# S4 convolution gated with a GLU on one core: second-half weights read again from the inputs, late sums gathered in SBUF, and a new order of issue

## The chip, the cores and the metric

The kernel runs on one core of one Trainium2 chip. The metric is the time on the device of one execution, in microseconds, as a median over several runs. All inputs lie in the chip's memory when the time starts, and the whole output must lie there when it ends. The program uses five engines that each work through their own instructions in order: TensorE (PE, matrix products), VectorE (DVE), ScalarE (ACT), GpSimd (POOL, which here only issues transfers that add to what is in memory) and SyncE (SP, which issues all other transfers). A wait at the head of an engine's queue holds up everything behind it on that engine.

## The reference, cut to what matters

```python
x = A_u                                            # 1 x 2048 x 512
g = sigmoid((x * gate_w).sum(-1, keepdims=True))   # one gate per row
a = _A_ref(x, ...)     # S4: K[d, l] = Re sum_n C dt B exp(dt A l), then a causal convolution of x with K, + x * Dskip
b = _B_ref(x, ...)     # GLU: h = sigmoid(x Wg) * (x Wu), 512 -> 1792; b = h Wd, 1792 -> 512
return g * a + (1 - g) * b
...
def _B_ref(x, w_gate, w_up, w_down):
    g = einsum("bsd,df->bsf", x, w_gate)
    u = einsum("bsd,df->bsf", x, w_up)
    h = sigmoid(g) * u
    return einsum("bsf,fd->bsd", h, w_down)
```

## The kernel before, in words

All products keep nearly float32 accuracy: a float32 matrix is split into a high part that TensorE takes as it is (fp32r) and a low rest, and three products (high by high, high by low, low by high) take the place of one. `split` (L938) does it for one 128x512 piece: SP loads the piece into a buffer of the pool ST, ACT copies the high part (L946), DVE subtracts it to get the low part (L947).

**The GLU.** The 2048 rows are taken in two halves of 1024; each half is two blocks of 512 rows (`sb`). The 1792 inner columns are 14 slices of 128 (`f`), taken in four groups of 3, 4, 4 and 3 (`GROUPS`). `hidden` (L1025) makes for each half, block and slice two products into PSUM (tile gups, L1040, 24 matmuls of 128x512); `post` (L1077) takes the sigmoid (ACT, L1081), the product (DVE, L1083) and splits the result (ACT L1087, DVE L1088). `down` (L1093) multiplies a group of slices with the down weights (tile dps, L1110) for each of the 16 row tiles `t`; `add` (L1120) scales the sum of the group by 1 - g on ACT (tile part, L1124) and sends it to the output: the first group by a plain store on SP (L1127), the other three by a transfer on POOL that adds to what is there (L1129). A tile's buffer comes free when its transfer has landed.

The weights are loaded and split in the first half (`load_gu` L967, `load_dn` L998). Three slices of the gate and up weights (`KEEP`) and of the down weights stay in SBUF for the second half, which takes the slices in reverse. The other 11 slices are stored after their split to a scratch tensor wsp in memory (`keep`, L956), 1024 KB of gate and up weights and 512 KB of down weights each, and the second half loads them from there, already split (L993, L1020).

**The convolution.** ACT and DVE build the tables from which the convolution's kernel is made: sines and cosines (`angles` L473, `powers` L441), exponentials (`magnitudes` L492) and doubling by complex products (`double` L520, L533 to L535). `tables` (L539) multiplies them on TensorE (tile kps, L577; 16 blocks of 128 small matmuls), `second` transforms the result (wps, L607) and stores it. `rows` (L629) transforms the input. `passes` (L697) then runs twice, for the first and the second 256 of the 512 output columns (`j` = 0, 1): `ustep`, `kstep` and `inverse` (tiles s2u, s2k, ips) make the product in the transformed domain, `evict` copies it out and stores it to b_s, and `finals` and `last` (L851, L866) load it again, transform it back (fps, L876), take sums and differences on DVE, scale by g on ACT (L901) and add the result to the output with a transfer on POOL (L905). Once the tables are done, some of their memory joins the pools of the second pass (L711 to L714).

**The order.** Every engine's instruction stream is written out by a planner while the program is built: each piece of work is a generator, and the string `ORDER` (L63) names, letter by letter, whose turn is issued next and on which engine ("tables PE", "splitw DVE", "add POOL"). So `ORDER` fixes the order on every engine; the cost figures in the planner only decide which free buffer is taken.

Of the kernel before, what the change touches and what calls it, by code (L numbers as in the profile page):

```python
# [44 lines left out]
GROUPS = [3, 4, 4, 3]  # L45
HALF = L // 2
# [10 lines left out]
         "rows PE", "hidden PE", "down PE", "passes SP", "split ACT", "split DVE", "keepw SP", "splitw ACT",  # L57
         "splitw DVE", "keepd SP", "splitd ACT", "splitd DVE", "second DVE", "second -", "second PE", "second ACT",
         "second SP", "sort ACT", "dot DVE", "dot ACT", "urest ACT", "urest DVE", "urest SP", "post ACT",
         "post DVE", "add ACT", "add SP", "add POOL", "ustep -", "ustep PE", "ustep ACT", "ustep DVE",  # L60
# [3 lines left out]
    "ABBDcEEdGDfgZfBcdgZZZGVWqrWqrWqrWqXDcdZZXVrFAYVEfDcgdZEZDfgZcdsZHvHIJwIGsECDijNOKfgKLYVFEvcPNZZfgMZvdwwKiDcWqZZWjZqdDaWq"  # L64
    "vwvwFuMWqheXuPZPucdZPQZaMMvwZMKEEijaZuRRXQVMSeFQrsuZxrSSvwZZfEESQSfSKraSQyviwsuuZaZYVSNOPSsuaxyageSNPvSSKSgZSaaZvLPMxauK"
    "ZePMsMZaayuSwvSSYVSfEfMwWWSWTExUZZvZwvgjgGWuQMwqqKfRRZwvQhQQQTZpZvguEfEsgMfUNOsqPSpNPSZSZZwSgZvSPaSaaZwZSZqSyeSPQuHSwSvw"
    "xaZfEaaSklmRSRQQSQQuxaZnaSZaNOfEvwyvwZSZrxaZFZPauNgSanSyvwFijHPvSZPwTZfiXxUZjvPQeZhEEvZwIwRvJXVIuRQQQZQZwZYyFpaaasvZZviw"
    "vfNOPTwjafKNKLMKuGxzUhygZZPMPgZeZZwtogMPuMQgMKvwpaaaaEeMSkSSKSVSYSKRRSQSSEvZZQSQSSQfxzaaaZaSNlSHvZuEfsxzaaaaOuVSwWrsmPNx"
    "zaWaafaHEZWqSvSSwZLSTnhxzUuZeWPvqgPMKZPMMwvgQpZRaaaaRqwqXwQQQZQTgMxzMNuKnofgvZZhOEEUZPNpkaaaaMSwvZuhSSZPvwSZXSlmZZZPPSwS"
    "vxzaaQFZZfRRSSwSfgSSQQSFijvaaFuFQQSwvZZeNESrVnOnoivYwZiZZPsuSuNSZSvSTvewZwgExzPEifPZPjUQpZjvRaajwaaxzgIJhwIhHRQKQQsuQNKL"  # L70
    "vwuZOaaaaxzTVvfgZaaaaEZxzUYMfKZgPNZvpMaZMPhakaatwlMPPMtZxzQaaaKwMSSSSSSuaHmfKgRSKxzaauaSRQQuuSZZDDavwSnnDvwQcZxzadLMKara"
    "SQSNOobbbbbbDcdavrMZZxzaaZvFaaMPc0SwFvZZ1bbMZNPSZPSSPSSwSvTijMKxzwijdw2cUQv245abbRZbRbFbdw6bZZvZZQQDMvDQDQTwpDUNwrijSZOP"
    "4NSScdSp6aaSbc5SZbb6SZPPZbPQklSSvwZxzavZaSwSaR67mZRQQxzcacnaSZQSQSvaSn8v!Z!$$xzaaaNZOPZSdvNSSSTwd0xPdZw!!$$z1bbPPUpZaaaQ"
    "ZIR3JoZ345bbbwbxzbaaabv4IKKZERwQLbxzaavMQQvZQNTOKaPZ5bhxU6MzZvEwN6MpaaaZP6PMPMxklmaaaZwQZvKMSSS6nSSSwSn78wKSSRSbZ!b!$$Zx"
    "aaaSZRQrxvQaaQ0wvQ!wS!Zva1bbw$xZZ2ZvNOSaPwZ$KaSvZyFy245bbbb4ZbZbawbyEESNPvSPSZSwZLMSTvKP6wxUyMovM5bbbM6pQR6RZZa6Z78!ZwQM"
    "vZ!$$rQQQNaaTZvxUOPKNZMSSSSSSZwvpaaaPSPwPwSZvZzQ#Sklvxaa#w0$SamRSZxRSQQyEnnZaQFSwyQvZN$a1bbZwry2vaFx24ZFZvZwZ5bbSbaZZOP4"
    "wvSaNwPPaS6SS6PvSZTaZExz56UQp6bRERQQQ7QZaaaax8!!$$ZvwTaaaaZxovUw#ypkl!$$zZmnnaZaZv9999%aawwo9b999%bbZZx&ab)bb0)b)ZbabaaZ"
    "Z(&)(*Z*(bzb(xaa**aba)19z9vwb99%bbvwEvZZvZw)wxa2zaa2(45bb40b(6vw*ZaxZ65bbbz*(v(*z6&)))bbbZZ6Zvwa(F(**b*a1F9939bwZZZZ7(9("
    "**vwvw2a8F!!$$b#4ZaxFvZvw!$wv5baZb0Z%b66wa4&)b))56b6b$EbZaax(Zv(**b((**bzbazba1a2baxz3456wv7aabaa8!xz!$6!b0$Zaa4Z!b$$b56"
    "6ab7aZ1xzaw22aabax8!#!!ab4a566b4EaazZvx$b$566aa$aZax78z!w#Z$ZaE#$a$!vzaa$wZZ$FFZ99999vwZZxza%vwZvZ&w(9ZZav))((**9w9(%&)Z"  # L80
    "Fa)9vZ(**9)xZzw9a(a99%a&)(**(99(*x*a)z9%)&)(v(*Zv*a(w(**)ax)wZZZ(a(*Z*vw(v(*awva*azxawzaaaaaaaxaxazxzzaxz")

XLATE = 0
SLACK = dict(dma=1.6, eng=0.06)
FETCH = 6.5

# [1114 lines left out]
```

## Time and profile before

| | |
|---|---|
| median of 3 runs (653.32 to 656.91) | 654.02 us |
| the profiled execution | 657.56 us |
| its span, first to last instruction | 655.8 us |
| mean granted clock of TensorE | 0.971 |

The span is counted from the first to the last instruction of the profiled execution; 1.76 us of its time lie around it. Busy time of an engine is the time in which at least one of its instructions runs. A duration in a row is from the start of one instruction to its end, and neighbours overlap a little, so the distance between two starts is what one costs in a row of them. In the rows of a timeline the bracket at the end is the idle time before the instruction and what ended it. "wgu", "wdn" and "xt" are inputs, "wsp" is the scratch tensor.

### The profile page before, as it was taken

The page shows a single profiled execution, that of the slowest core. Times are in us where ns is not written, and L with a number is a line of the kernel's source. Part 1 is how long each engine was busy: PE and PEld are TensorE (multiplying, and loading weights), DVE is VectorE, ACT ScalarE, POOL GpSimd, SP SyncE. Part 2 cuts the span into 40 slices and gives each one's busy share as a digit, 9 for nine tenths or more (in the row PEclk, how much of TensorE's full clock was granted, in tenths as well). Part 3 has the DMA queues.
Part 4 walks back from the last instruction along what each step waited for, and adds up shares of the span by engine and source line. Part 5 has one row for each costly group of instructions (what it writes and reads, how often), then busy time and mean ns, then how long its engine had stood idle before and what let it go on. Part 6 is the DMA issues. An engine that isn't in the chain of part 4 may idle for free.

```text
span 655.8 us, 16738 instructions
## 1 busy us (share of the span) xinstructions
PE 599.2 (91%) x7136; PEld 454.4 (69%) x7136; DVE 518.2 (79%) x726; ACT 444.3 (68%) x668; POOL 70.3 (11%) x84
## 2 busy tenths in 40 slices
PE   3987989989989999998999999999799889899993
PEld 2564778867868787866777777777677557567672
DVE  6999999999999998999999999897324636452450
ACT  4696888988799889987988879876352232322341
POOL 0000000000100011100111000000013301311363
PEclk9799989999999999997999999999899989999997
DMA  7585581668828686964389469186599999999988
GB/s 239 173 320 182 196 275 65 198 219 252 224 69 244 226 225 163 246 132 122 49 188 278 98 172 335 37 250 184 162 258 252 263 286 230 241 296 262 247 108 115
DMA packets 96586, 132.50 MB, mean 202 GB/s; under 512 B 39936, under 2 KB 65408, under 8 KB 92672
## 3 DMA queue, kind: packets, MB, share of 16 engines
q1 hardware_dynamic: 84992, 114.65, 58.0%
q0 software_dynamic: 11520, 16.78, 17.5%
q8 instruction: 56, 0.92, 0.6%
q14 instruction: 18, 0.15, 0.1%
HBM read 67.97 MB, written 63.44 MB: 200 GB/s over the span
## 4 chain that ended last, share of the span: by engine, by line
PE 45%; DVE 17%; issue 12%; DMA 11%; ACT 6%; SPq 4%; POOL 4%; POOLq 0%; DVEq 0%; ACTq 0%
PE gups L1040 23%; PE dps L1110 11%; PE kps L577 4%; POOL out L905 3%; PE wps L607 2%; PE s2k L788 2%; DMA out<-mn 2%; DMA u<-xp 2%; DMA ak<-a_k 1%; DMA out<-part 1%; DMA out<-yt 1%; DVE t L533 1%; DVE sg L1083 1%; DVE T L535 1%; DVE T L534 1%
## 5 line engine op out<-in xcount | busy, mean ns | idle before, releaser
L1040 PE MATMUL gups<-x,gu 128*128 128x512 f32 x1344 | 341.0, 401 | 19.4 <-ACT gu L946 6.3
L1040 PEld LDWEIGHTS gups<-x,gu 128*128 128x128 f32 x1344 | 253.0, 192 | 92.5 <-issue 15.0
L1110 PE MATMUL dps<-dnw,h 128*128 128x512 f32 x672 | 174.3, 397 | 2.9 <-ACT part L1124 1.3
L1110 PEld LDWEIGHTS dps<-dnw,h 128*128 128x128 f32 x672 | 125.2, 189 | 38.9 <-issue 7.0
L1129 POOL DMA_DIRECT2D out<-part x48 | 42.6, 888 | 482.9 <-ACT part L1124 337.3
L1124 ACT ACTIVATE part<-dps,omg 128x512 f32<-128x512 f32 x64 | 43.6, 681 | 63.7 <-PE dps L1110 60.9
L1083 DVE TENSOR_TENSOR sg<-gups,sg 128x512 f32<-128x512 f32 x56 | 38.4, 687 | 22.0 <-PE gups L1040 19.9
L506 ACT ACTIVATE B<-B 128x32 f32<-128x32 f32 (+2 forms) x96 | 53.7, 673 | 0.3
L577 PE MATMUL kps<-B,T 128*32 128x64 f32 x2048 | 35.6, 231 | 15.3 <-DVE B L515 8.1
L577 PEld LDWEIGHTS kps<-B,T 128*32 128x32 f32 x2048 | 32.7, 118 | 22.2 <-issue 8.0
L1087 ACT ACTIVATE h<-sg 128x512 fp32r<-128x512 f32 x56 | 34.9, 626 | 16.5 <-DVE sg L1083 16.2
L533 DVE TENSOR_TENSOR t<-T,bz 128x1024 f32<-128x1024 f32 (+3 forms) x48 | 41.3, 861 | 1.5 <-ACT ez L436 0.9
L1088 DVE TENSOR_TENSOR h<-sg,h 128x512 fp32r<-128x512 f32 x56 | 38.4, 687 | 4.9 <-ACT h L1087 4.9
L535 DVE TENSOR_TENSOR T<-T,t 128x1024 f32<-128x1024 f32 (+3 forms) x48 | 41.4, 863 | 0.2
L534 DVE TENSOR_TENSOR T<-T,bz 128x1024 f32<-128x1024 f32 (+3 forms) x48 | 41.5, 864 | 0.0
L1081 ACT ACTIVATE sg<-gups 128x512 f32<-128x512 f32 x56 | 33.0, 593 | 6.5 <-DVE h L1088 4.2
L616 ACT ACTIVATE kev<-wps 128x1024 f32<-128x1024 f32 x16 | 31.0, 2006 | 5.5 <-PE wps L607 5.5
L798 DVE TENSOR_TENSOR tt<-s2k,uf 128x1024 f32<-128x1024 f32 x16 | 19.6, 1225 | 18.4 <-PE s2k L788 18.3
L431 ACT ACTIVATE af<-ex 128x1024 int32<-128x1024 f32 x16 | 16.9, 1059 | 13.3 <-DVE ex L484 13.3
L788 PE MATMUL s2k<-ak,wwk 64*32 64x256 f32 x512 | 19.2, 397 | 5.7 <-DVE ev L309 3.2
L901 ACT ACTIVATE yt<-yt,g 128x256 f32<-128x256 f32 x16 | 7.4, 502 | 24.7 <-DVE yt L894 24.7
L309 DVE COPY yt<-fps 128x512 f32<-128x512 f32 x7 | 4.8, 692 | 24.1 <-PE fps L876 17.3
(102 smaller groups left out, 730.8 us busy)
## 6 DMA issues: line engine op xcount, KB each, us to landing
out<-part POOLq DMA_DIRECT2D x48, 256.0 KB, 5.5
wsp<-gu SPq DMA_DIRECT2D x11, 1024.0 KB, 6.6
gu<-wsp SPq DMA_DIRECT2D x11, 1024.0 KB, 8.4
a_u<-evu SPq DMA_DIRECT2D x32, 256.0 KB, 4.8
a_k<-kev SPq DMA_DIRECT2D x8, 1024.0 KB, 6.7
au<-a_u SPq DMA_DIRECT2D x32, 256.0 KB, 6.6
ak<-a_k SPq DMA_DIRECT2D x32, 256.0 KB, 5.1
b_s<-ev SPq DMA_DIRECT2D x32, 256.0 KB, 4.3
```

Source lines behind the costliest of these rows:

```text
L506: A.activation(B[:, :, 0, 1 << k::2 << k], B[:, :, 0, 1:64 >> k:2], AF.Exp, scale=float(1 << k))
L533: yield "DVE", dve(n), lambda: V.tensor_tensor(t2, src, sb, op=OP.mult), [t, slot.t]
L534: te = yield "DVE", dve(n), lambda: V.tensor_tensor(dst, src, br, op=OP.mult), [t]
L535: te = yield "DVE", dve(n), lambda: V.tensor_tensor(dst, dst, t2[:, :, ::-1], op=OP.add), [te]
L577: mm(p[32 * jj:32 * jj + 32, s], T[:, 32 * i + ch, c], B[:, ch, c], start=(c == 0), stop=(c == 1), tile_position=(0, 32 * jj), skip_group_ ...
L1040: mm(p, gu[:, a, k, dc], x[:, b, dc], start=(dc + n == 0), stop=(dc == NC - 1 and n == 2))
L1083: t = yield "DVE", dve(512), lambda: V.tensor_tensor(sg, pu, sg, op=OP.mult), [t, tu]
L1087: t = yield "ACT", act(512), lambda: A.activation(h[:, 0], sg, AF.Copy), [t, hs.t]
L1088: t = yield "DVE", dve(512), lambda: V.tensor_tensor(h[:, 1], sg, h[:, 0].bitcast(F32), op=OP.subtract), [t]
L1110: mm(p, h[:, a, 128 * s:128 * s + 128], dn[:, b], start=(f == fs[0] and n == 0), stop=(f == fs[-1] and n == 2))
L1124: te = yield "ACT", act(512) + 0.1, lambda: A.activation(part, p, AF.Copy, scale=omg[:, t:t + 1]), [tp, gate[t, 1].t, ss.t]
L1129: ts = yield "POOL", kb(430), lambda: nc.gpsimd.dma_start(out[t], part, accum_op=OP.add), [te, begun[t]]
```

## The change

Four things are done together.

1. `keep` is gone, and so is wsp. In the second half the 11 slices that are not kept are loaded from the inputs again, three pieces of 256 KB a slice, and go through `split` as in the first half. `drop` no longer waits for a store.
2. For the row tiles 8 to 15 (the second half) a new generator `take` loads the output tile into an SBUF buffer `acc` once the first two groups and the first 256 columns of the convolution have been added in memory. The last two groups (`INTO` = 2) are then added to `acc` by one DVE instruction each, from PSUM, and the second 256 columns of the convolution by one DVE instruction for each tile. SP stores the finished tile. For these, the ACT scaling and the POOL transfer are gone. The other 32 + 24 POOL transfers stay.
3. The tables' memory joins the pools as several buffers rather than one each: TA as 2, KEV and EX as 2 each, KST as 2 buffers of ST, TB as the 8 buffers `acc`.
4. `ORDER` is a new string. The figures with which the planner counts transfers are new too.

```diff
+class Piece:
+    def __init__(self, slot, n, i): self.slot, self.n, self.i = slot, n, i
...
-                for n, s in (("big", TB[0]), ("big", KEV[0]), ("big", EX[0]), ("uf", TA[0]), ("ev", T2[0]), ("t", T2[1]),
-                             ("wwk", PG[0]), ("wwu", PP[0]), ("wwv", BZ[0])):
+                for n, s in (("ev", T2[0]), ("t", T2[1]), ("wwk", PG[0]), ("wwu", PP[0]), ("wwv", BZ[0])):
                     fin[n].join([s])
+                fin["uf"].join(pieces(TA[0], 2, [P, 2, 2, 2, W]))
+                fin["big"].join(pieces(KEV[0], 2, [P, 4, W]) + pieces(EX[0], 2, [P, 4, W]))
+                ST.join(pieces(KST[0], 2, [P, 512]))
+                ACC.join(pieces(TB[0], 8, [P, D]))
...
+    out_done = [Ev(INTO + 1) for _ in range(NM)]
+    held = [[Ev(), None] for _ in range(NM)]
+    oleft = [Ev(len(GROUPS) - INTO + 1) for _ in range(NM)]
+    late = lambda j, t: t >= 8 and j == NW - 1
+    def take(t):
+        yield out_done[t]
+        sl, = yield ACC, 1
+        a = held[t][1] = sl.tile("acc")
+        held[t][0].set((yield "SP", kb(256), lambda: S.dma_start(a, out[t]), [out_done[t].t, sl.t]))
+        yield oleft[t]
+        sl.free((yield "SP", kb(256), lambda: S.dma_start(out[t], a), [oleft[t].t]))
+
+    def gather(t, add, n, deps, slot):
+        yield held[t][0]
+        a = held[t][1]
+        te = yield "DVE", dve(n) + 0.06, lambda: add(t, a), deps + [held[t][0].t]
+        if slot is not None:
+            slot.free(te)
+        oleft[t].set(te)
...
             for t in range(4):
-                yield begun[4 * t4 + t]
+                yield held[4 * t4 + t][0] if late(j, 4 * t4 + t) else begun[4 * t4 + t]
...
+            if late(j, 4 * t4):
+                for i in range(2):
+                    yield from gather(4 * t4 + k[i], lambda t, a: V.scalar_tensor_tensor(
+                        a[:, cols], y[:, i], g[:, t:t + 1], a[:, cols], op0=OP.mult, op1=OP.add), W, [te], slot if i else None)
+                continue
...
-    def keep(done, stored, dst, src, size):
-        yield done
-        stored.set((yield "SP", (kb(size), 0.18 - 6e-5 * size), lambda: S.dma_start(dst, src), [done.t]))
...
-                else:
-                    yield wsent[f]
-                    t = yield "SP", (kb(1024), 0.1), lambda: S.dma_start(gf, ga), [gs.t, wsent[f].t]
...
+                for k in range(2):
+                    yield from split("splitw", wgu[f, :, 512 * k:512 * k + 512], gu[:, 0, k], gu[:, 1, k], gs, wready[half, f][0][k])
...
-                    dready[1, f][0].set((yield "SP", kb(512), lambda: S.dma_start(df, da), [ds.t, dsent[f].t]))
...
+                yield from split("splitd", wdn[f], dn[:, 0], dn[:, 1], ds, dready[half, f][0])
...
         yield gate[t, 1] if gi == 0 else added[t][gi - 1]
+        if t >= 8 and gi >= INTO:
+            yield from gather(t, lambda t, a: V.scalar_tensor_tensor(
+                a, p, omg[:, t:t + 1], a, op0=OP.mult, op1=OP.add), 512, [tp], bank)
+            added[t][gi].set(tp)
+            return
```

The two `ORDER` strings are too long to print. This is what they say of the turns that come before the last "tables PE" (the sixteenth block of small matmuls, kps), and of the whole string; turns that are not named have the same count in both.

| turn | ahead of the last kps, before | after | whole string, before | after |
|---|---|---|---|---|
| hidden PE (6 matmuls of 128x512) | 177 | 180 | 228 | 228 |
| down PE (3 matmuls of 128x512) | 148 | 144 | 224 | 224 |
| splitw ACT and DVE, each | 28 | 39 | 28 | 50 |
| splitd ACT and DVE, each | 14 | 18 | 14 | 25 |
| post ACT / post DVE | 85 / 83 | 86 / 85 | 112 / 112 | 112 / 112 |
| urest ACT / urest DVE (128x1024) | 13 / 3 | 16 / 0 | 13 / 3 | 16 / 0 |
| ustep ACT / ustep DVE (128x1024) | 6 / 2 | 8 / 0 | 12 / 4 | 13 / 3 |
| evict ACT / evict DVE (128x512) | 12 / 2 | 15 / 1 | 25 / 7 | 24 / 8 |
| add ACT | 43 | 42 | 64 | 48 |
| add POOL / last POOL | 25 / 0 | 26 / 0 | 48 / 32 | 32 / 24 |
| take SP, add DVE | 0 | 0 | 0 | 16 each |

ACT holds one set of functions at a time: sine, exponential and sigmoid are in three sets, copy and absolute value are in all. Followed through the strings, the ACT turns change from one set to another 58 times in the order before and 70 times in the order after, in both strings ahead of the last kps.

More of the change, by code (lines that the diff above doesn't have):

```diff
@@ L56 @@
          "mags DVE", "mags ACT", "tables DVE", "tables -", "tables PE", "rows -", "rows SP", "rows DVE",
[L57 to L60, printed above, removed]
+         "rows PE", "hidden PE", "down PE", "passes SP", "take SP", "split ACT", "split DVE", "splitw ACT",
+         "splitw DVE", "splitd ACT", "splitd DVE", "second DVE", "second -", "second PE", "second ACT", "second SP",
+         "sort ACT", "dot DVE", "dot ACT", "urest ACT", "urest DVE", "urest SP", "post ACT", "post DVE",
+         "add ACT", "add SP", "add POOL", "add DVE", "ustep -", "ustep PE", "ustep ACT", "ustep DVE",
          "kstep -", "kstep PE", "kstep DVE", "inv -", "inv PE", "finals SP", "evict ACT", "evict DVE",
@@ L161, in __init__ @@
     def __init__(self):
-        self.free, self.kind, self.last, self.strands, self.dma, self.adds = dict(SP=0.74, ACT=0.7, DVE=0.87), None, None, [], 0.0, 0.0
-        self.count, self.entered = 63.0, 0.0
+        self.free, self.kind, self.last, self.strands = dict(SP=0.74, ACT=0.7, DVE=0.87), None, None, []
+        self.count, self.entered, self.used = 63.0, 0.0, [0.0] * 1024
     def spawn(self, gen, kind):
@@ L298, in body @@
     dts = dr.tile([16, 32], F32, name="dts")
-    wsp = dr.tile([NF, P, 3072], F32, name="wsp")
     cst = ctx.enter_context(pool("cst"))
@@ L313, in body, with pieces @@
     XB = slots(ps, "xb", BANKS["xb"], [P, 2, 512])
+    def pieces(slot, n, shape):
+        parts = Slots(Slot(Piece(slot, n, i), None, shape, F32) for i in range(n))
+        for s in parts:
+            s.t = slot.t
+        return parts
     def release(slot, ev):
```

128 lines of the change are left out of this document (63 added, 65 removed).

## The prediction

> **What bounds the kernel now.** I begin with the page's summary and its slices.
>
> ```profile
> span 655.8 us, 16738 instructions
> PE 599.2 (91%) x7136; PEld 454.4 (69%) x7136; DVE 518.2 (79%) x726; ACT 444.3 (68%) x668; POOL 70.3 (11%) x84
> PE   3987989989989999998999999999799889899993
> DVE  6999999999999998999999999897324636452450
> ACT  4696888988799889987988879876352232322341
> DMA  7585581668828686964389469186599999999988
> ```
>
> Two parts can be seen. Up to slice 28, some 460 us, DVE is full, PE nearly so, and the transfers have gaps. Behind it DVE and ACT are half idle and the transfers fill every slice. The border is the last block of the tables' small matmuls (kps). The timeline shows it, and the view by stages, split there, puts numbers to the parts (columns: PE, PEld, DVE, ACT, POOL busy, clock, DMA share, GB/s). The next lines, on the transfers from 470 us on, say which queue fills them.
>
> ```profile
> 469.62 0.33 PE L577 MATMUL kps<-B,T 128*32 128x64 f32 x9 [3.97 <-issue]
> 0.00:470.00 470.00, 434.43 (x5451) 336.63 (x5452) 438.88 (x620) 384.68 (x565) 22.96 (x30) 0.98 0.66 192
> 470.00:656.00 186.00, 164.78 (x1686) 117.82 (x1686) 79.35 (x106) 59.59 (x103) 47.34 (x54) 0.95 1.02 228
> q1 hardware_dynamic: 35168, 32.25, 64.7%
> q0 software_dynamic: 7776, 9.96, 36.3%
> ```
>
> First part: DVE is idle 31.1 us of 470, so it sets this part's end, and ACT has 85.3 us to spare. Second part: SP's queue (q1) and POOL's adding transfers (q0) together take 101% of the 16 DMA engines. PE is the engine with most work there. What stopped it is the next question, answered by the waits of PE in that part, with two waits of DVE and ACT that stand ahead of them, the half-clock place in the timeline, and the tail.
>
> ```profile
> PE s2k L788 <- DVE ev L309: 3.2, 1, 3.2
> PE s2k L788 <- ACT ev L309: 2.1, 1, 2.1
> PE fps L876 <- DMA b_in<-b_s: 0.6, 2, 0.3
> PE dps L1110 <- DMA dnw<-wsp: 0.4, 1, 0.4
> PE s2k L788 <- DMA ak<-a_k: 0.4, 1, 0.4
> DVE ev L309 <- DMA out<-mn: 9.2, 1, 9.2
> ACT ev L309 <- DMA out<-mn: 6.1, 2, 4.1
> 536.68 1.96 PE L788 MATMUL s2k<-ak,wwk 64*32 64x256 f32 x32 [3.17 <-DVE ev L309]
> 540.02 4.01 PE L1040 MATMUL gups<-x,gu 128*128 128x512 f32 x12
> 545.53 1.07 PE L788 MATMUL s2k<-ak,wwk 64*32 64x256 f32 x32
> 637.55 6.87 PE L1110 MATMUL dps<-dnw,h 128*128 128x512 f32 x29 [0.23 <-DVE h L1088]
> 645.10 0.69 ACT L1124 ACTIVATE part<-dps,omg 128x512 f32<-128x512 f32 x1 [1.94 <-DMA out<-part]
> 649.31 0.87 POOL L1129 DMA_DIRECT2D out<-part  x1 [0.42 <-issue]
> ```
>
> The five waits of PE, 6.7 us, all have a late transfer behind them: the copies "ev" could not start because a buffer was held by an adding transfer (out<-mn) for 9.2 and 6.1 us. After the 3.17 us pause the s2k block took 1.96 us where the next took 1.07, and twelve matmuls at 540.02 took 4.01 us where a row below has 2.72. So the clock was halved from the pause to about 543 us, some 6.8 us, of which I count half as lost, 3.4 us (an estimate). Together 10.1 us are due to transfers. Then the tail: the last matmul ends at 637.55 + 6.87 = 644.4, the span at 655.8, 11.4 us later, since the last sums wait for a buffer (1.94 us) and then queue on POOL until 649.31.
>
> **The change part by part.** These rows give the prices: a matmul in a row of them, the split's two instructions, the copies that change their engine, the transfers.
>
> ```profile
> 454.04 2.72 PE dps L1110 x12
> L947 DVE TENSOR_TENSOR gu<-st,gu 128x512 fp32r<-128x512 f32 x28 | 19.0, 685 | 0.0
> L946 ACT ACTIVATE gu<-st 128x512 fp32r<-128x512 f32 x28 | 17.3, 626 | 1.7 <-issue 1.1 <-DMA st<-wgu 0.5
> 630.50 0.69 DVE L888 TENSOR_TENSOR mn<-fps,yt 128x512 f32<-128x512 f32 x1
> 631.10 0.68 DVE L889 TENSOR_TENSOR mn<-fps,yt 128x512 f32<-128x512 f32 x1
> L309 DVE COPY evu<-ups 128x1024 f32<-128x1024 f32 x3 | 3.7, 1219 | 0.0
> L309 ACT ACTIVATE evu<-ups 128x1024 f32<-128x1024 f32 x13 | 13.2, 1017 | 7.0 <-PE ups L661 7.0
> gu<-wsp SPq DMA_DIRECT2D x4, 1024.0 KB, 9.4
> dnw<-wsp SPq DMA_DIRECT2D x7, 512.0 KB, 7.4
> out<-part SPq DMA_DIRECT2D x16, 256.0 KB, 4.4
> out<-part POOLq DMA_DIRECT2D x8, 256.0 KB, 4.7
> L1081 ACT ACT_TABLE_LOAD x18 | 23.1, 1283 | 0.3
> 125.75 1.28 ACT L1081 ACT_TABLE_LOAD   x1
> 127.04 0.60 ACT L1081 ACTIVATE sg<-gups 128x512 f32<-128x512 f32 x1
> ```
>
> A matmul costs 2.72 / 12 = 0.227 us. A DVE instruction of 128x512 lasts 0.69 and starts 0.60 after its neighbour (630.50, 631.10), so I price it at 0.60, one of 128x1024 at 1.22 - 0.09 = 1.13, and an ACT copy of 128x512 at 0.626 - 0.09 = 0.53.
>
> *First part, DVE.* Counted in the order, 15 splits more stand ahead of the last kps: 15 x 0.60 = +9.0; two post turns more, +1.2; three urest and two ustep copies go to ACT, -5 x 1.13 = -5.7; one evict less, -0.6. Sum **+3.9 us** on the engine that sets the end of this part. Bounds: 0, if the 31.1 us of idle take it in, and +9 if the copies that leave gain nothing because DVE only waits there instead.
>
> *First part, ACT.* 15 splits x 0.53 = 8.0; five copies x 0.93 = 4.6; three evicts, one post, less one add, 1.6; and twelve more changes of function set at 1.283: 15.4. That is 29.6 us, from 384.7 to 414 of 470. I take **0**: 56 us of idle remain to cover it. If the cover is gone, DVE waits behind it; this is the third rival. The row speaks of what stands in front of the loads, 0.3 us of idle for 18, and the timeline of what follows: load at 125.75, sigmoid at 127.04. The Trainium skill (ScalarE: Activation LUTs, section "What ACT_TABLE_LOAD costs") also gives 1283 ns but adds a drain of about 1380 ns, 2.66 us a switch. By it the twelve switches would be 31.9 us, by the rows 15.4; the rows leave no gap for a drain, so the measurement decides.
>
> *First part, PE.* Ahead of the last kps three hidden turns more and four down turns less: 18 - 12 = 6 matmuls, which leave the second part: **-1.4 us** (0 to -1.4).
>
> *First part, stores.* 11 x 1.5 MB of stores to wsp vanish, on a DMA share of 0.66. DVE waits for hardly any transfer there, so 0.
>
> *Second part, transfers.* POOL loses 16 x 256 + 8 x 128 KB, 5.24 of its 9.96 MB: 36.3% x 0.53 = 19 points. The loads from wsp in this part (4 of gu, 7 of dnw: 7.9 MB) come to half: 3.9 / 32.25 x 64.7 = 8 points less. `take` adds 16 x 256 KB, 4.2 MB: 8 points more. So 101% fall to about 82%. Of the 10.1 us due to transfers I take two thirds away, **-6.7 us**, since the adds of the first 256 columns, which held "ev", stay on POOL. Bounds: 0 (the buffer is held just as long) and -10.1.
>
> *Second part, engines.* DVE gets 18 splits, 16 sums from PSUM and 8 of 128x256; the new instruction's nearest row is the 128x512 sum from PSUM above, so 34 x 0.60 + 8 x 0.33 = 23 us, on 79 of 186. PE, busy 164.8 of 186, covers that; uncovered it would be up to 23. ACT loses 16 scalings and gains 18 splits: even.
>
> *New waits.* Each sum of `gather` waits on DVE for the load of `take`, and behind it stand the products of `post`, for which PE's banks wait. The load can go out when three adds have landed. Seven of the eight loads stand at least 9 PE turns ahead of their sums in the order; the last add, load and sum stand at one place, 29 PE turns ahead of the end. I take 0, since queues may run ahead of the order's places; the bound is the landing of an add and of a load, 4.7 + 4.4 = 9.1 us, once. SP loses 22 stores and 22 loads and gains 33 loads and 16 takes: +5 issues, nothing.
>
> *Tail.* After the last dps come one DVE sum (0.7), an SP store (4.4 to landing) and what closes the program, which before took 655.8 - 649.31 - 4.7 = 1.8 (4.7 is the median landing of a POOL add in the last 56 us). With 0.2 to start, 7.1 in place of 11.4: **-4.3 us** (bounds 0, as some POOL adds still stand among the last turns, and -5.5).
>
> *Sum:* +3.9 + 0 - 1.4 - 6.7 - 4.3 = **-8.5 us** on the profiled execution, 657.56, of which the span is 655.8 and 1.76 lie around it: 649.1. The runs' median, 654.02, is 3.5 below that execution, so the forecast is **645.5 us**.
>
> **The rivals.** *All the waits go* (chance 0.21): with a fifth of the transfers gone, the five waits and the half clock vanish, and the 31.1 us of idle DVE in the first part take in its 3.9 us. -1.4 - 10.1 - 4.3 = -15.8: 638.2. For it speaks the full DMA row; against it that DVE was 93% busy.
>
> *Hidden anyway* (0.19): the waits for "ev" come from the buffer and not from the load on the DMA engines, and only the tail is gained: +3.9 - 1.4 - 4.3 = -1.8: 652.2. For it speaks that both waits name out<-mn, whose transfers of the first 256 columns stay.
>
> *ACT becomes the bound of the first part* (0.18): the twelve set changes fall between an ACT step and a DVE step of the same chain (sine, exponential, doubling), so each holds DVE by its 1.283 us. -8.5 + 15.4 = +6.9: 660.9. It turns the result slower when 11.8 of the 15.4 us are exposed. For it: DVE's waits for ACT were there before,
>
> ```profile
> DVE bz L466 <- ACT ey L461: 4.9, 3, 2.9
> DVE B L511 <- ACT B L506: 3.3, 2, 2.5
> ```
>
> against it: ACT waited far longer for DVE and PE, 85.3 us idle.
>
> **How the numbers follow.** The forecast has 0.42, the rivals 0.21, 0.19 and 0.18. A measurement of this kernel tells about 0.5% from no change: 650.75 to 657.3. Faster: forecast and first rival, 0.63; same: 0.19; slower: 0.18. The range goes to the first rival with its tail at the bound and some DVE idle gained, 633, and to the slower rival, 660, leaving out about one tenth on each side. The likeliest cases of one sign, 633 to 650.7, hold 0.6.
>
> **What would show it.** After: kps ends 2 to 6 us later than 470; DVE's waits for ACT ahead of it stay under 16 us; about 70 table loads; DMA share behind it near 0.85; the waits of s2k for ev shorter than 3.2 and 2.1 and the half clock gone there; last matmul to end of span about 7 us. Wrong if kps comes 10 us later with DVE idle for ACT (third rival), if the ev waits stay at 5 us (second), if DVE waits at the new sums for acc, or if the new order moves the border by more than its counts do: the counts say what is issued before what, not how well it interleaves, and that is the largest thing the trace of before cannot show.

## The result and the profile after

The changed kernel takes **632.9 us** (median; 630.66 to 635.37) against 653.67 (652.95 to 656.91) for the kernel before on the same chip: a ratio of 0.968, 95% interval 0.963 to 0.972. It is some 21 us faster where 8.5 were forecast, just past the low end of the range. A later set of runs (e14 below) gave 0.962 (0.956 to 0.967).

The profiled execution took 631.64 us. These lines of its page answer to those shown of before: the span, the busy times and the slices.

```profile
span 629.9 us, 16805 instructions
PE 594.3 (94%) x7136; PEld 449.9 (71%) x7136; DVE 543.2 (86%) x777; ACT 466.7 (74%) x695; POOL 49.4 (8%) x60
PE   4999899999979999996999999999999999989996
DVE  6899999999999999999999999999743767746467
ACT  4698989999998899999899899996943424321140
DMA  7714324247834754493786976732799999995985
```

The shape is the same: DVE full up to slice 28, the transfers nearly full behind it. PE does the same 7136 matmuls, but it starts at full pace in the second slice rather than the third and has fewer holes. To compare, I cut each execution at the start of the last kps block (the border) and at the end of the last matmul. The view by stages gives, for before and then for a second profile of it (e1 below): columns are PE, PEld, DVE, ACT and POOL busy, clock, DMA share, GB/s.

```profile
0.00:65.00 65.00, 46.90 (x252) 32.19 (x253) 57.49 (x113) 43.66 (x77) 0.20 (x4) 0.94 0.69 227
65.00:463.80 398.80, 385.30 (x5075) 302.46 (x5073) 380.00 (x506) 340.81 (x489) 22.76 (x26) 0.98 0.66 185
463.80:644.40 180.60, 167.00 (x1815) 119.80 (x1814) 80.74 (x108) 59.12 (x103) 44.74 (x51) 0.97 1.01 236
```

```profile
460.80:644.90 184.10, 169.62 (x1815) 119.99 (x1814) 80.72 (x108) 58.91 (x103) 44.73 (x51) 0.96 1.02 232
```

For the changed kernel, and a second profile of it (e14):

```profile
0.00:65.00 65.00, 55.48 (x271) 40.73 (x271) 55.84 (x106) 48.07 (x76) 0.20 (x4) 1.00 0.52 160
65.00:458.60 393.60, 378.09 (x5059) 293.28 (x5057) 382.63 (x523) 364.54 (x525) 22.75 (x26) 0.99 0.58 147
458.60:624.70 166.10, 160.68 (x1809) 115.86 (x1808) 102.85 (x148) 54.14 (x95) 26.42 (x30) 1.00 1.00 218
```

```profile
459.20:627.80 168.60, 162.12 (x1809) 116.74 (x1808) 103.01 (x148) 54.27 (x95) 26.40 (x30) 0.99 0.97 214
```

The spans are 655.8 and 655.1 before, 629.9 and 633.0 after; the tail is what is left of each behind the last matmul. So, with the mean of two profiles each:

| stage | forecast | before (two profiles) | after (two profiles) | change of the means |
|---|---|---|---|---|
| first part, to the border | +3.9 | 463.8, 460.8 | 458.6, 459.2 | -3.4 |
| second part, to the last matmul | -8.1 (-6.7 and -1.4) | 180.6, 184.1 | 166.1, 168.6 | -15.0 |
| tail | -4.3 | 11.4, 10.2 | 5.2, 5.2 | -5.6 |
| sum | -8.5 | | | -24.0 |

The medians differ by 20.8 us in the first set of runs and by 27.3 in the later one; the sum of the stages, from two profiles each, lies between. Every stage came out better than forecast: the first by 7 us, the second by 7, the tail by 1.

**The second part** can be taken apart from those rows. PE's idle time is the length less the busy time: 13.6 and 14.5 us before, 5.4 and 6.5 after, so -8.1. The rest is busy time, -6.9: 6 matmuls left this part (1815 to 1809), 1.4 us, and the clock rose from 0.97 and 0.96 to 1.00 and 0.99, worth 0.035 x 182 - 0.005 x 167 = 5.5 us (an estimate: the missing share of the clock times the length). The waits of PE behind the border in the changed kernel are few; these are the three largest (us in total, times, longest):

```profile
PE fps L934 <- DMA b_in<-b_s: 1.7, 2, 1.2
PE s2u L797 <- ACT ev L335: 1.5, 1, 1.5
PE s2k L824 <- DMA parts<-a_k: 0.7, 1, 0.7
```

The pause of 3.97 us with the cause "issue" inside the last kps block, which the prediction quoted and then did not count, is not there. The queues from 459 us on:

```profile
q1 hardware_dynamic: 37477, 31.83, 78.2%
q0 software_dynamic: 4464, 4.98, 19.3%
```

POOL's adding transfers fell from 9.96 to 4.98 MB as counted. But the two queues together still take 98% of the 16 engines in a stretch of 171 us: the work for the transfers fell from 1.01 x 186 = 188 us to 167, and the part shrank with it.

**The first part** was forecast to end later because DVE gets more work there. Its instructions ahead of the border rose by 10 (113 + 506 = 619, then 106 + 523 = 629), 11 by the count in the order. But its idle time fell from 463.8 - 437.5 = 26.3 us to 458.6 - 438.5 = 20.1, its busy time rose by 1 us where 3.9 were forecast, and the first 65 us hold 5 to 9 us more of PE's work (46.9 before and 48.9 in e1, 55.5 after and 54.3 in e14). The waits of DVE and ACT in this part say where the idle time went; first two of ACT's before (DVE's largest two, 4.9 and 3.3 us, stand in the prediction), then after.

```profile
ACT af L431 <- DVE ex L484: 13.3, 7, 4.3
ACT af L435 <- DVE ex L432: 9.3, 7, 2.9
```

```profile
DVE B L544 <- ACT B L539: 5.4, 2, 4.2
DVE sg L1116 <- PE gups L1073: 2.9, 1, 2.9
DVE gu L1011 <- ACT gu L1010: 2.2, 1, 2.2
...
ACT af L464 <- DVE ex L517: 4.6, 6, 2.3
ACT af L468 <- DVE ex L465: 3.3, 4, 1.9
```

ACT, in the chain of sines and exponentials (af, ex), waited 22.6 us for DVE before and 7.9 after, while it took on 12 more changes of function set (59 table loads in the trace of before, 71 after) and its busy time up to the border rose by 28 us (384.5 to 412.6). DVE's two largest waits for ACT come to 8.2 us before and 7.6 after.

**The tail**: the last sums are three DVE instructions in a row, and the last store follows.

```profile
623.64 1.07 PE L1143 MATMUL dps<-dnw,h 128*128 128x512 f32 x4
...
624.50 2.07 DVE L1156 SCALAR_TENSOR_TENSOR parts<-dps,omg,parts 128x512 f32<-128x512 f32 x3
```

The last matmul ends at 624.7, the last sum at 626.6, the span at 629.9. SP's stores of the finished tiles land within 2.1 us (median of 8):

```profile
out<-parts SPq DMA_DIRECT2D x8, 256.0 KB, 2.1
```

### The profile page after: what moved, and what is told of

Same layout as the page of the kernel before. It is cut to its first block, busy times and chain, and to the rows that moved or that the text cites. A ratio compares the mean times of both kernels' runs of the same rounds, so it can differ in the third digit from the quotient of the medians.

```text
span 629.9 us, 16805 instructions
## 1 busy us (share of the span) xinstructions
PE 594.3 (94%) x7136; PEld 449.9 (71%) x7136; DVE 543.2 (86%) x777; ACT 466.7 (74%) x695; POOL 49.4 (8%) x60
## 4 chain that ended last, share of the span: by engine, by line
PE 48%; DVE 23%; DMA 11%; ACT 8%; SPq 4%; issue 4%; POOL 0%; DVEq 0%; POOLq 0%
PE gups L1073 26%; PE dps L1143 12%; PE kps L610 3%; DVE t L566 2%; DVE T L567 2%; DMA b_in<-b_s 2%; DVE T L568 2%; PE wps L640 2%; PE s2k L824 2%; ACT B L539 2%; DMA parts<-a_u 2%; DVE B L548 1%; DMA parts<-wdn 1%; DVE B L544 1%; PE ips L859 1%
## 5 line engine op out<-in xcount | busy, mean ns | idle before, releaser
L1167 POOL DMA_DIRECT2D out<-part x31 | 27.7, 892 | 439.8 <-ACT part L1162 421.2
L1162 ACT ACTIVATE part<-dps,omg 128x512 f32<-128x512 f32 x47 | 31.9, 678 | 16.8 <-PE dps L1143 10.2
L1011 DVE TENSOR_TENSOR gu<-st,gu 128x512 fp32r<-128x512 f32 x48 | 32.7, 687 | 8.5 <-ACT gu L1010 8.5
L1010 ACT ACTIVATE gu<-st 128x512 fp32r<-128x512 f32 x48 | 29.5, 624 | 5.0 <-DMA st<-wgu 5.0
L335 ACT ACTIVATE ev<-ips 128x512 f32<-128x512 f32 x24 | 13.6, 595 | 21.8 <-PE ips L859 10.3
L1156 DVE SCALAR_TENSOR_TENSOR parts<-dps,omg,parts 128x512 f32<-128x512 f32 x16 | 11.8, 747 | 18.2 <-PE dps L1143 11.8
```

What stands on the lines that cost most here:

```text
L1011: te = yield "DVE", dve(512), lambda: V.tensor_tensor(lo, st, hi.bitcast(F32), op=OP.subtract), [te]
```

## The experiments

Ratios are to the kernel before on the same chip. Where an edit changes the number of turns, a new `ORDER` had to be fitted to it by moving turns about until the planner's own count of the end fell no more. Such an order may be worse than it need be, so what e5, e6 and e8 lose can be more than their edits cost. This holds for e5 to e11, e13 and e15; e1 to e4, e12 and e14 keep an order as it was, and e16 moves one turn. A profile is of one execution, which need not be a typical one of its kernel; where it lies far from the median, the text says so.

**e1: the kernel before once more**, for what recurs in its profile.

> The kernel before, unchanged, profiled once more: its first profiled execution (657.56 us) was the slowest of its runs, and the terms of the sum were taken from it. If the pauses of PE of that execution belong to the kernel (4.0 us in the last kps block, 3.2 and 2.1 us before s2k, half clock from 536 to 543 us), they are there again within 1 us. If they were an accident of that execution, the span is some 4 us shorter, near 652, and one of them is missing.

One run, 656.91 us. The border came 3 us earlier (460.8), and PE's waits behind it were others:

```profile
PE kps L577 <- issue: 4.4, 1, 4.4
PE fps L876 <- DMA b_in<-b_s: 3.8, 5, 2.0
PE s2u L761 <- DMA au<-a_u: 3.3, 4, 1.6
```

The waits for "ev", 5.3 of the 6.7 us on which the forecast for this part rested, are gone here, and the part is no shorter: other late transfers take their place. So these two profiles share late transfers as the kind of wait, but not the places where they are waited for. What recurs at the same place is the pause "issue".

**e2 and e4: more work for DVE in the first part**, in the kernel before and in the changed one: 16 instructions of 128x512 more, whose results are overwritten.

```diff
 # magnitudes(), first DVE turn
+V.tensor_tensor(B[:, :8, 1], rb, rb, op=OP.mult)   # rb = re[:, :8, None].to_broadcast([P, 8, 64])
```

> The kernel before with one more DVE product of 128x512 in each of the 16 groups of exponentials of the first part, 16 x 0.60 = 9.6 us of DVE; its result is overwritten. If DVE sets the end of the first part (93% busy there), as the prediction had it, the last kps block and the whole come 8 to 10 us later. If DVE's idle time (26.5 us up to the last kps) takes it in, both move by under 3 us.

> The changed kernel with the same 16 DVE products, 9.6 us of DVE in the first part. If DVE sets the end of the first part here too (20 us idle of 459), it is 8 to 10 us longer. If PE, 94.5% busy up to there, has taken its place as the bound, it moves by under 4 us.

e2: 1.0096 (1.0047 to 1.0144). e4: 0.969 (0.965 to 0.974). The stages of e2, then of e4:

```profile
0.00:467.30 467.30, 436.56 (x5322) 337.32 (x5322) 446.38 (x634) 384.69 (x565) 22.95 (x30) 0.98 0.66 190
467.30:643.90 176.60, 166.88 (x1815) 118.75 (x1814) 80.72 (x108) 59.10 (x103) 44.70 (x51) 0.98 1.05 241
```

```profile
0.00:465.20 465.20, 434.53 (x5328) 333.61 (x5328) 447.72 (x644) 412.89 (x600) 22.96 (x30) 0.99 0.56 147
```

DVE's busy time rose by about 9 us in each. The border went from 463.8 and 460.8 to 467.3 in the one and from 458.6 and 459.2 to 465.2 in the other, 5.0 and 6.3 us from the means: over half of what is added to DVE there is paid, less than the 8 to 10 us expected and more than the 3 or 4 of the other theory. So the prediction's premise holds in the main: DVE sets this part's end, though not to the full. As a whole e2 is some 6 us slower; e4 lies 0.5 points above the mean of the changed kernel's two ratios (0.9646), some 3 us, within the intervals. And e2's second part is 176.6 us with the very same instructions on PE: its last kps block runs without the pause.

**e3: twelve more changes of ACT's function set in the order before**, as many as the new order has, six sines of one column put between exponentials.

```diff
 # magnitudes(), second ACT turn
+gi in (2, 4, 6, 8, 10, 12) and A.activation(dum[:, :1], dum[:, :1], AF.Sin)
```

> The kernel before with a sine of 128x1 put between the exponentials of 6 of the 16 groups, so that ACT changes its function set 12 times more: 12 x 1.283 = 15.4 us and six short instructions, some 17 us of ACT in the first part, as many changes as the new order adds. If ACT has room (85 us idle in the first 470), the time moves by under 3 us. If each change holds DVE, as the prediction's third rival had it, it is 12 to 17 us longer.

1.0156 (1.0086 to 1.0225), some 10 us (6 to 15 by the interval) for 12 x 1.283 = 15.4 us of loads. DVE's wait for ACT in the doubling, 3.3 us before, is now:

```profile
DVE B L513 <- ACT B L508: 14.9, 8, 2.8
```

11.6 us more. So idle time of ACT, 85 us in this part, is no cover at the place where a load stands between an exponential and the product that needs it. This is the third rival's mechanism, and it works. The changed kernel doesn't pay it: its order has the 12 changes, and the wait there is 5.4 us.

**e5: the stores and reloads of wsp back** in the changed kernel (`load_gu`, `load_dn`, `keep`, `drop` and `split` as in the kernel before), and **e13: the stores alone**, which nobody reads; the second half still loads from the inputs and splits, and a buffer comes free when its store has landed.

```diff
 # e5 and e13, half 0 (in short)
+plan.spawn(keep(done, sent, ga, gf, 1024), "keepw")    # 512 KB in load_dn
+plan.spawn(drop(gs, wready[half, f][2], sent), "free")
 # e5 alone, half 1
-yield from split("splitw", wgu[f, :, ...], gu[:, 0, k], gu[:, 1, k], gs, wready[half, f][0][k])
+t = yield "SP", (kb(1024), 0.1), lambda: S.dma_start(gf, ga), [gs.t, wsent[f].t]
```

> The changed kernel with part 1 undone: the split weights are stored to scratch memory in the first half and loaded from there in the second; the order is that of the changed kernel, with the turns of the stores and loads fitted in. If the gain comes from the order and the pauses of PE that it removes, the time stays within 6 us of the changed kernel (633 to 639). If the transfers of part 1 are what the gain is made of, most of the 21 us is lost again: 645 or more, with the DMA share of the first part back at 0.66 and longer pauses of PE behind the last kps.

> The changed kernel with the 22 stores to wsp put back (11 of 1024 KB, 11 of 512 KB, all in the first part) though nobody reads them; a weight buffer is again free only after its store has landed; the second half still loads from the inputs and splits. The order is fitted again. Theory A (the prediction's step 'First part, stores': 0): the last kps starts within 2 us of the changed kernel's 458.6, and the whole stays within 3 us of it, 630 to 636. Theory B (the stores held the border): the last kps starts 3 us or more later, as with all stores and reloads back (461.9), the part behind it stays at 166 us, and the whole is 636 to 640.

e5: 0.984 (0.980 to 0.988). e13: 633.96 us, 0.968 (0.963 to 0.973). The second parts, e5 and then e13, and under them PE's waits in e5:

```profile
461.90:643.70 181.80, 167.69 (x1809) 119.81 (x1808) 92.70 (x130) 45.32 (x77) 26.43 (x30) 0.94 0.95 219
```

```profile
462.30:626.10 163.80, 158.82 (x1809) 116.15 (x1808) 103.39 (x148) 55.39 (x96) 26.40 (x30) 1.00 0.98 217
```

```profile
PE dps L1175 <- DMA dnw<-wsp: 4.2, 3, 3.6
PE fps L934 <- DMA b_in<-b_s: 3.2, 4, 1.0
PE gups L1105 <- DMA gu<-wsp: 2.2, 1, 2.2
```

The stores cost little: the border comes 3 us later, as in e5, and the second part takes it back; two profiles of the kernel before lie as far apart at the border, so these 3 us are not clear of the scatter. In the same set of runs e13 lies 4 us above e14, with intervals that overlap. The reloads cost 18 us of second part by these two profiles, half of it as idle PE and half as a clock of 0.94 behind the pauses. But e5's profile is of the slowest of its four runs and e13's of the fastest of its four: by the ratios the two kernels are 11 us apart, by the medians 13.

**e12: the same bytes without the wait.** In the changed kernel each of the 33 loads of 256 KB in the second half is followed by a copy of the same size from memory to memory that nobody waits for. A reload moves the high and the low part, twice the bytes of a load, so this makes up the difference in bytes read.

```diff
 # split(), half 1 only
-lambda: S.dma_start(st, src)
+lambda: (S.dma_start(st, src), again and S.dma_start(twin[next(twins)], src))
```

> The changed kernel, in which each of the 33 loads of weights of the second half is followed by a copy of the same 256 KB from the input to scratch memory that nobody reads or waits for: the bytes that the loads of already split weights had, without their effect on buffers. If the bytes set the second part, it loses most of the 16 us that it lost with the stores back: 642 or more. If it was the latency of the large loads into the few weight buffers, it stays within 4 us of 633.

0.972 (0.965 to 0.978), 639.7 us, between the two expectations. The second part:

```profile
461.80:638.00 176.20, 166.31 (x1809) 118.95 (x1808) 103.03 (x148) 54.15 (x95) 26.47 (x30) 0.97 0.97 233
```

By this one profile that is 9 us over the mean of the changed kernel's two (167.4), where e5 is 14 over it. By the ratios, against the mean of the changed kernel's two (0.9646), e12 loses 0.7 points, some 5 us, and e5 1.9, some 13 us. So the bytes look like a third to two thirds of what e5 loses, but e12's profile is of the slowest of its four runs, and its interval overlaps those of the changed kernel: that the bytes cost anything is not clear of the noise. That they are not all of it is: 17 of the 33 copies are issued behind the border, and with them e12 moves more there than e5 (41.0 MB against 39.9) in 5.6 us less. The other part fits the way in which a reload comes: 1024 KB at once, landing a median of 8.2 us after issue in e5, into a buffer that must be free first, where a split has its 256 KB in another pool by then. A poorer order in e5 would look the same, so that part is argued, not shown. (The copy also writes its bytes, so as a measure of the reads alone it is high.)

**e6: part 2 taken back** in the changed kernel: all late sums through ACT and POOL again.

```diff
-INTO = 2
+INTO = 4
-late = lambda j, t: t >= 8 and j == NW - 1
+late = lambda j, t: False
```

> The changed kernel with part 2 undone: all late sums go by ACT and adding transfers on POOL again, the rest and the order as in the changed kernel, with the turns concerned fitted in. The prediction's tail and second part say: tail 11 us in place of 5, and up to 6 us more of waits behind ev, so 639 to 645. If the order is all, the tail alone comes back: 637 to 640.

1.0008 (0.9968 to 1.0048), 656.93 us: all of the gain gone, and more than either theory expected. The second part, and the last adds on POOL:

```profile
458.00:630.80 172.80, 163.90 (x1809) 117.27 (x1808) 91.53 (x127) 68.52 (x119) 40.51 (x46) 0.99 1.03 210
```

```profile
632.65 0.86 POOL L1167 DMA_DIRECT2D out<-parts  x1 [0.27 <-issue]
...
638.65 0.86 POOL L1167 DMA_DIRECT2D out<-part  x1 [0.68 <-issue]
640.15 0.86 POOL L1167 DMA_DIRECT2D out<-parts  x1 [0.63 <-issue]
642.52 0.87 POOL L1167 DMA_DIRECT2D out<-part  x1 [1.50 <-issue]
```

The last matmul ends at 630.8, the span at 649.0: the adds leave POOL one every 1.6 us or so, and eight of them stand behind the end of PE's work. Against the changed kernel's profiles the tail is 13 us longer, which is this queue, and the second part 5. This profile is of the fastest of ten runs, 6 us below their median, so some 6 of the 24 us lost stand in no stage shown here. The kernel before, whose order puts its last sums further ahead, has a tail of 11, so an order with a shorter tail exists for POOL's sums; part 2 may well be worth less than e6 says.

**e7: the tables' memory as single buffers** (part 3 taken back for TA, KEV, EX and KST).

> The changed kernel with part 3 undone but for the eight acc buffers: TA, KEV and EX join their pools as one buffer each, KST not at all; order as in the changed kernel with SP's turns fitted in. The prediction gave the buffers nothing; by that the time stays within 3 us of 633. If the second pass lives on having two uf and four more big buffers, PE waits for s2u and s2k come back behind the last kps: 640 or more.

0.968 (0.964 to 0.971), 636.68 us: nothing that is clear of the noise, as the prediction left it out of the sum.

**e8 to e11, e15: the pieces apart.** e8 is the kernel before with the changed kernel's order, carried over turn by turn; e9 has part 1 alone and e10 and e15 part 2 alone, in the order before as far as the turns allow; e11 is the kernel before with its own order fitted again with the new planner figures.

> The kernel before (stores, POOL sums, single buffers) with the order of the changed kernel, the turns that it lacks fitted in. If the order makes the gain, it is near 636 to 642, and the last kps comes near 459 as in the changed kernel. If the parts make it, it is near the kernel before, 650 to 657.

> The kernel before with part 1 alone: no stores of split weights, the second half loads the inputs again and splits; sums and buffers as before; the order is that of the kernel before, with the new turns fitted in and turns moved until the planner's own count fell no more. If part 1 is worth in the old order what its undoing cost in the new (some 11 us), it is near 643 to 648 and the second part (last kps to last matmul) is near 170 us instead of 180. If it only pays together with the rest, 650 to 657.

> The kernel before with part 2 alone: the last sums of the second half kept in SBUF by DVE; stores, loads and buffers as before; order of the kernel before with the turns fitted in the same way. If the tail is all that part 2 gains by itself, the end of the last matmul to the end of the span falls from 11 to about 5 us and the time to 647 to 651. If the loss of 20 us in its undoing was its worth and not that of an ill fitting order, it is below 645.

> Part 2 alone in the order before (the last two groups' sums and the last 16 column blocks of the convolution gathered in SBUF; stores and reloads stay), once more, since the first profile of it was a disturbed one. Theory A (part 2 is worth the tail and nothing else in the order before): 4 us from the last matmul to the end against 11.4, 179 to 182 us of second part, ratio 0.985 to 0.992. Theory B (it also shortens the second part, since the adding transfers are what PE waits for there): second part 172 to 176, ratio 0.975 to 0.982.

> The control for the two others: the kernel before, all parts as before, with the planner's new figures for transfers and its own order fitted with the same number of moves. If fitting the order does the work, it falls by as much as the kernels with one part alone. If the parts do it, it stays within 4 us of 654 to 657.

| kernel | median us | ratio (95%) | border / second part / tail |
|---|---|---|---|
| e8, order alone | 668.54 | 1.016 (1.012 to 1.020) | 463.9 / 184.1 / 18.2 |
| e9, part 1 alone | 658.34 | 1.005 (1.000 to 1.010) | 466.7 / 181.3 / 9.4 |
| e15, part 2 alone | 653.51 | 0.994 (0.990 to 0.998) | 467.6 / 179.3 / 3.9 |
| e11, before, fitted again | 665.83 | 1.011 (1.006 to 1.016) | 471.6 / 196.3 / 10.9 |

e10 is the same kernel as e15, run earlier: 652.91 us as the median of four (642.67 to 655.17), against 657.31 for the kernel before. e11's profiled execution took 680.55 us, 15 more than its other three runs, so its stages are read with care. No piece gives the gain alone, and the sum of their effects is a loss. But e11 is the control: fitting its own order again, with no part changed, made the kernel before 1.1% slower. Against that control part 1 alone is 0.6 points faster, within the intervals, and part 2 alone 1.7, so some of what the parts give may be hidden by orders that are worse than the one before. Part 2 alone has the short tail (3.9 us) but gives most of it back at the border; part 1 alone shortens the tail by about 1 us and neither of the other stages, and the pause "issue" stands in its last kps block again:

```profile
PE kps L610 <- issue: 4.7, 1, 4.7
```

**e14: the changed kernel once more.**

> The changed kernel once more, to see how far the three parts recur in a second profiled execution. If they do: last kps at 457 to 460, 165 to 168 us from there to the last matmul, 5 us of tail, 630 to 636 as a whole. If the early border was an accident of the one profiled execution: last kps at 461 to 464 as in the kernel before.

629.86 us, 0.962 (0.956 to 0.967); its stages stand in the section on the result. The border and the tail recur (459.2 and 5.2 us), the second part nearly (168.6).

**e16: the last kps block one PE turn later** in the kernel before, and nothing else.

```diff
-"...ZxovUw#ypkl!$$zZmnna..."    # U is "tables PE", Z is "hidden PE"
+"...Zxovw#ypkl!$$zZUmnna..."
```

> The kernel before with its last kps block issued one turn later on PE, behind the 6 matmuls of the next 'hidden PE'; nothing else. In three profiles of the same PE stream the pause with the cause 'issue' (3.6 to 4.4 us) stands between the 119th and the 120th matmul of that block. Theory A (the pause belongs to a place in PE's instruction stream, so it comes from fetching instructions): it now stands after the 113th matmul of the block, 6 earlier, and the time stays within 0.5% of the kernel before. Theory B (it belongs to the block's work or data): it stays at the 119th. Theory C (it comes from the moment, other transfers at that time): it goes, the half clock behind it too, and the kernel is 4 to 6 us faster.

651.88 us, 0.993 (0.990 to 0.996). PE's timeline there, first in e1, then in e16:

```profile
460.80 1.88 PE L577 MATMUL kps<-B,T 128*32 128x64 f32 x119
467.09 0.48 PE L577 MATMUL kps<-B,T 128*32 128x64 f32 x9 [4.42 <-issue]
467.50 2.93 PE L1040 MATMUL gups<-x,gu 128*128 128x512 f32 x6
```

```profile
459.98 2.88 PE L1040 MATMUL gups<-x,gu 128*128 128x512 f32 x12
462.79 1.99 PE L577 MATMUL kps<-B,T 128*32 128x64 f32 x128
465.81 1.87 PE L607 MATMUL wps<-wk,kst 32*64 32x128 f32 x113 [1.03 <-DVE kst L594]
468.62 0.48 PE L607 MATMUL wps<-wk,kst 32*64 32x128 f32 x15 [0.94 <-issue]
```

The block now runs through; after it PE waits 1.03 us for DVE, and a pause of 0.94 us with the same cause stands in the next block of small matmuls. The six matmuls of gups behind the pause in e1 take 2.93 us, as long as twelve in e16: the granted clock is 0.50 for 6.8 us around the end of the pause. Moving one turn saves about 4.5 us (2 to 7 by the interval): the pause does not come from the work in the block, and an order can avoid it without any of the changes.

What PE waits for there can be seen in the DMA queues. One of them, of kind "instruction", carries 16 KB a time; the page of the kernel before counts 56 of its transfers (then MB and share):

```profile
q8 instruction: 56, 0.92, 0.6%
```

PE has 7136 matmuls and as many weight loads, 255 of these instructions for each transfer. In the kernel before a transfer of this queue runs from 467.26 to 468.22 us, inside the pause, which begins at 465.65 and ends at 469.62. In e1, e3, e8 and e9 it is the same: the transfer starts after PE has stopped, and PE goes on 1.3 to 1.5 us after its end. In e2 and e16, which don't stop there, the last one ahead of that place had landed before the block began (464.4 against 467.35 in e2). So PE stands still because its next instructions are not there yet. Why the transfer comes late is not shown: in e1 the transfers filled all 16 engines up to the pause (a share of 1.05), in e2 the transfer came after a stretch without any, and no run changes that alone.

## Why the prediction was wrong

**First part, DVE, +3.9: wrong, by 7 us.** The count was right (10 instructions more, 11 forecast), and the premise held in the main (e2, e4). DVE's busy time rose by 1 us rather than 3.9; the rest is idle time. What failed is the lower bound: "0, if the 31.1 us of idle take it in". An engine that sets a stage's end and still idles 26 us can lose part of that idle time, so the bound had to reach below nothing. With the new order PE does more of its work in the first 65 us, and DVE idles 6 us less (4.5 by the means of two profiles). The prediction's last sentence named this as what the trace of before cannot show, but the range gave it only what "some DVE idle gained" covered.

**First part, ACT, 0: right in number, but its reason is not enough.** ACT's busy time rose by 28 us, 29.6 were forecast. That 56 us of idle time remain is no cover by itself; e3 shows about two thirds of such loads exposed when they fall into the chain. The new order has its extra loads where ACT used to wait for DVE: ACT's waits in the chain of sines fell by 14.7 us, about the 15.4 us that the loads take. That the one filled the other fits the rows; no run shows it by itself. The forecast that DVE's waits for ACT stay under 16 us held.

**First part, stores, 0: right within the scatter** (e13, whose border comes 3 us later).

**Second part, -6.7: a step that failed as far, by its size.** "Together 10.1 us are due to transfers" summed five named waits and one half-clock stretch. What PE lost there was 13.6 us of idle time and some 5 us by the clock (0.03 of 180.6), 19 us together. The change took away 13 to 14 of them. That this is again about two thirds is luck: the fraction was meant for late transfers, and the base left out the pause of 3.97 us and the 1.7 us lost by the clock behind it. The row of that pause stood in the prediction's second fence, but the view by stages was cut at 470, behind it, so that its 4 us counted as idle time of DVE in the first part (31.1 us; 26.3 up to the start of the block) and as nothing for PE. Some 3 us of smaller waits were left out too. e1 shows as well that the named waits were not the lasting ones. e5 shows that the second part grows again when the reloads come back (18 us against e13 by the profiles, 11 as a whole by the ratios), and e6 that it grows by 5 us with POOL's adds; each has an order of its own, and which of the two weighs more is not shown. e16 shows that the pause goes by order alone, with all transfers as they were; with its clock it stands for some 6 of the 15 us by which this part became shorter (an estimate: 3.97 + 1.7).

**Second part, PE, -1.4: right** (1815 to 1809 matmuls). **DMA share near 0.85: wrong.** The transfers still fill the part, since it became shorter as they became fewer. A full DMA row does not say by itself that PE waits for transfers: after the change it is at 1.00 and 0.97, with 5.4 and 6.5 us of PE's time idle.

**New waits, 0: nearly right.** DVE's 16 sums waited 6.3 us in all for the loads of `take`,

```profile
L1156 DVE SCALAR_TENSOR_TENSOR parts<-dps,omg,parts 128x512 f32<-128x512 f32 x16 | 11.8, 747 | 18.2 <-PE dps L1143 11.8 <-DMA parts<-out 6.3
```

and the prediction had named such waits as a sign of being wrong; but behind the border PE had one wait for such a sum, of 0.3 us in all.

**Tail, -4.3: right, 1 us short.** 7.1 us were forecast, 5.2 measured: three sums rather than one are among the last instructions, but the store landed in 2.1 us, not 4.4.

**The rivals.** "All the waits go" came nearest: 638.2, 5 us too slow, as its terms had the same base of 10.1 us and nothing below 0 for the first part. "Hidden anyway" falls by the second part and "ACT becomes the bound" by the border. What the three had in common was a fixed order, and that is what e8 to e11 leave open: whether the gain belongs to the parts or to the order can't be divided up, since each part alone, in an order not made for it, gives 0.6% or less, and the new order without the parts is 1.6% slower. Shown is that the pause goes by a move of one turn (e16), and that the whole loses some 2 points with the stores and reloads back (e5) and 3.6 with POOL's sums back (e6), each with an order fitted to it.

## What to carry to other kernels

When a change replaces a hand-fitted order, let the range of each stage reach as far below nothing as its bounding engine idles, and take as the base of a stage the whole of PE's idle time and of its lost clock (length less busy time, length times missing clock) rather than the waits that one profile happens to name. Read "issue" pauses as time to be gained: look when the transfers of the "instruction" queue land, and try to move a turn: one turn moved took such a pause away. Reloading data already split into high and low parts doubles the bytes. Loading the original and splitting it again, where ACT and DVE have idle time and the transfers have none, was worth some 11 to 13 us here within the whole change, and nothing by itself in the old order (e9).

## What the runs showed of the hardware

- PE paused 4.0, 4.4, 3.6, 2.9 and 4.7 us (before, e1, e3, e8, e9) with no releaser, in four of them behind the 119th of 128 small matmuls of the same block, and didn't in e2 with the same PE stream. In each a transfer of 16 KB of the "instruction" queue began only after PE had stopped, and PE went on 1.3 to 1.5 us after its end.
- These transfers come once in 255 of PE's instructions, that is 128 matmuls with their weight loads (56 for 14272). The pause that was left in e16 (0.94 us) stood just that far on in PE's stream: counted from the same place, 6 + 128 + 113 = 247 matmuls ahead of it, against 119. It ends 1.4 us after such a transfer (467.19 and 468.62).
- In these traces the granted clock falls to 0.50 for 3.4 us or a multiple of it (6.8 in before and e1, 13.7 in e7), the stretch at the end of a trace aside. One of 6.8 us began 2.3 us into the pause of e1, and one of 3.4 us 1.1 us after the end of the pause of before (470.7 against 469.6).
- SP's stores of 256 KB landed in 2.1 us (median of the last 8, after), where the 16 stores of the first group in the kernel before had taken 4.4.
- A function-set load of 1.28 us moved the end by some 0.86 us on average (0.5 to 1.2 by the interval) where it stood in the chain of the tables (e3: some 10 us for 12), though ACT was idle for 85 us of that part.
